# Attention over packed queries with a two-layer MLP: own PSUM tiles for copies on two engines, batch 1's p loaded apart, bias sums by 128x32 tiles, and another order of loads and work

## Chip, core and metric

The kernel runs on one core of a Trainium2 chip. The metric is the device time of one execution in microseconds (us); of the kernel before, three runs took 257.86, 258.21 and 258.63 us (median 258.21). The core has five engines that run side by side and wait for each other by semaphores: TensorE (PE, matrix products into PSUM; PEld is its loading of weights), VectorE (DVE), ScalarE (ACT), GpSimd (POOL) and SyncE (SP). Here GpSimd only makes one diagonal mask and issues loads, which turn float32 into bfloat16 on the way. SyncE issues stores and transposing transfers. In the profile "DMA" is the transfer engines.

## What is computed

There are 8 batches of 8 heads with 576 positions of 64 numbers, and 32 packed queries p per head. The packed queries attend over k and v; the 32 results of each head then serve as keys and values for q. The output, 4608 rows of 512, goes through an MLP with a squared ReLU.

```python
def sm_attn(qq, kk, vv):            # softmax(qq kk^T / 8) vv
    ...
p_packed = sm_attn(p, k, v)         # 8 x 8 x 32 x 64
x = sm_attn(q, p_packed, p_packed)  # -> 4608 x 512, heads side by side
h = x @ w_in                        # 512 -> 2048
r = np.maximum(h, 0.0)
g = s * (r * r) + b                 # s and b are single numbers
out = g @ w_out                     # 2048 -> 512
```

Since s and b are single numbers, the kernel computes `s * (r*r @ w_out) + b * colsum(w_out)`. The column sums of W_out times b are the tile `biasrep`, the same row in all 128 partitions.

## The kernel before

All products have bfloat16 operands. Every engine takes its instructions in the order in which the program names them (`Pinned`, line 67, and `mm` and `tr`, lines 61 and 64), so nearly all rows of the profile carry L62, L65 or L73, and one goes by the names of tiles. That order is a list of words written out by hand (line 609), which `run` (line 531) turns into calls. The words, with b the batch:

- `Lk`, `Lq`, `Lv`, `Lp`, `Lpall`, `Lwi`, `Lwo`, `Lsb`: loads of keys, queries, values, packed queries of batch 0, packed queries of batches 1 to 7, quarters of W_in and W_out, and s and b. All go through GpSimd's one queue, in this order. Batch 0 is loaded in halves of four heads ahead of the list (lines 586 to 596).
- `Tk`, `Tq` (`on_pe`, line 188): keys or queries of half the heads are transposed by TensorE into a PSUM tile and copied out by VectorE; for the last half of q of batch 0 ScalarE copies one half of the tile and VectorE the other. Only batches 0 and 1 go this way; later ones use a transposing transfer (`Dk`, `Dq`).
- `PD`, `PP` (`prep_p0`) and `PPA` (`prep_pall`): the packed queries are doubled, transposed and laid out block by block in `pbd`.
- `F` (`first_scores`), `V` (`order_v`), `P` (`packed`): scores of the packed queries and their exponentials, values in another order (`vr`), and the packed result with its sums in PSUM tile `pps`. At the end of the second half the result is rounded into `ppd` by four copies on two engines.
- `S`, `A`: scores of q against the packed results, exponentials `e`, and their division by their sums, which gives the weights `aT`.
- `W` (`packed_w`): the packed results times W_in, scaled into `pw`. The first MLP layer is then `aT` times `pw`. For batch 0 a word W takes one of four quarters of 512 columns.
- `M` (`mlp_in`), `h` (`mlp_in_half`): 128 columns of the first layer for a batch, or 256 for half of its rows; ReLU into `rlu` on ScalarE (a few on VectorE), squared by VectorE into `gT`.
- `B` (`bias_part`, line 437): products of W_out with a matrix of ones, added up over 16 blocks of rows; the last is multiplied by b into `biasrep`.
- `Ob.txn` (`Out.step`, line 460): n of the 16 products of output tile t, each 128x512; after the last, VectorE makes `ysb` from the sum, s and `biasrep`, and `store` (line 445) issues the stores on SyncE. The very last tile is done in two halves of columns.
- `Z` and `Y` (lines 513 and 520): products of zeros, which compute nothing.

PSUM has two pools: `psh` with two tiles of two banks (transposes, scores, first layer; rows hps) and `psy` with four tiles of one bank (outputs, packed results, batch 0's W, the bias sums, the zeros; rows yps, pps, wps, zps). A tile is free again once its last reader is done. A load waits for the landing of the load eight places earlier in GpSimd's queue, and for whatever still reads the buffer that it fills; there is one buffer each for k, q and v as loaded.

Of the kernel before, what the change touches and what calls it, by code (L numbers as in the profile page):

```python
# [14 lines left out]
def kernel(  # L15
# [79 lines left out]
    pn = constp.tile([P, 2, 2, D], BF16, name="pn")  # L95
    pall = constp.tile([16 * (B - 1), 16, 2, D], BF16, name="pall")
# [8 lines left out]
    onesb = constp.tile([P, P], BF16, name="onesb")  # L105
    zb = constp.tile([P, NB], BF16, name="zb")
# [15 lines left out]
    def load_p0():  # L122
        pool.dma_start(out=pn[:, :, 0, :], in_=p[0].rearrange("(x g) j d -> (g j) x d", x=2))

    def load_pall():
        pool.dma_start(
            out=pall[:, :, 0, :],
            in_=p[1:B].rearrange("b h (i t) d -> (b h i) t d", t=16),
        )
# [13 lines left out]
    def load_sb():  # L143
        pool.dma_start(out=svec[:], in_=moe_s[0:1].unsqueeze(0).to_broadcast([P, 1]))
        pool.dma_start(out=bvec[:], in_=moe_b[0:1].unsqueeze(0).to_broadcast([P, 1]))
# [7 lines left out]
    def prep_p0():  # L153
        pt = big(BF16)
        for x in range(2):
            tr(
                pt[:, 0, x * P:(x + 1) * P],
                pn[:, x, :, :],
                identb[:],
            )  # L160
        for c2 in range(2):
            act.copy(
                out=pbd[D * c2:D * c2 + D, :, 0, :, c2, :],
                in_=pt[D * c2:D * c2 + D, 0, 0:2 * P].rearrange("p (g a j) -> p a g j", g=4, a=2),
            )

    def prep_pall():
        twice(pall)
        n = 16 * (B - 1)
        pt = big(BF16)  # L170
        for t in range(16):
            tr(
                pt[:, t // 8, (t % 8) * P:(t % 8) * P + n],
# [3 lines left out]
        src = pt[:].rearrange("p i (t n) -> p (i t) n", n=P)[:, :, 0:n].rearrange(  # L177
            "p t (x a i) -> p a x i t", a=2, i=JJ
        )
        for c2 in range(2):  # L180
            for a in range(2):
                out = pbd[D * c2:D * c2 + D, a, 1:B, :, c2, :].rearrange("p b g (i t) -> p (b g) i t", i=JJ)
                if c2:
                    act.copy(out=out, in_=src[D * c2:D * c2 + D, a])
                else:
                    vec.tensor_copy(out=out, in_=src[D * c2:D * c2 + D, a])

    def on_pe(b, what, half):
# [3 lines left out]
        tp = big(BF16)  # L192
        for h4 in range(4):
            for cp in range(CP):
                o = (h4 % 2) * HS + cp * R
                tr(
                    tp[:, h4 // 2, o:o + R],
# [4 lines left out]
        if b == 0 and what == "q" and half == 1:  # L202
            act.copy(out=d[:, 0], in_=tp[:, 0, 0:2 * HS])
            vec.tensor_copy(out=d[:, 1], in_=tp[:, 1, 0:2 * HS])
        else:
            vec.tensor_copy(out=d, in_=tp[:, :, 0:2 * HS])
# [40 lines left out]
    def packed(b, half):  # L247
        if half == 0:
# [21 lines left out]
        if half == 0:  # L270
            return
        pd = ppd[b % 2]
        src = pp[:, 0:HP * 2 * NP].rearrange("p (g a j) -> p a g j", g=HP, a=2)
        rd[b] = smp.tile([P, 2], F32, tag="rd", name="rd")
        vec.reciprocal(out=rd[b][:], in_=sums)
        for a in range(2):
            vec.tensor_copy(out=pd[D * a:D * a + D, a], in_=src[D * a:D * a + D, a])
            act.copy(out=pd[D - D * a:2 * D - D * a, a], in_=src[D * a:D * a + D, a])
        rs[b] = smp.tile([P, 2], F32, tag="rs", name="rs")
        vec.tensor_scalar_mul(out=rs[b][:], in0=rd[b][:], scalar1=scale)  # L280
# [68 lines left out]
    def packed_w(b, chs):  # L349
        if chs[0] == 0:  # L350
# [94 lines left out]
    def store(ysb, d0, d1, i0, b, col, n):  # L445
        rows = out[b * S:(b + 1) * S, :].rearrange("(r c) d -> c r d", c=NC)
        end = i0 + n
        while i0 < end:
            x, r0 = divmod(col, R)
            m = min(R - r0, end - i0)  # L450
            sp.dma_start(out=rows[chunk(x), r0:r0 + m, d0:d1], in_=ysb[i0:i0 + m, d0:d1])
# [3 lines left out]
    class Out:  # L455
# [4 lines left out]
        def step(self, n):  # L460
# [16 lines left out]
            if m1 == NFF:  # L477
# [5 lines left out]
                for b, col, n in self.parts:  # L483
                    store(self.ysb, d0, d1, i0, b, col, n)
# [46 lines left out]
    def run(word):  # L531
# [9 lines left out]
        elif what == "Lp":  # L541
            load_p0()
# [8 lines left out]
        elif what == "PD":  # L551
            twice(pn)
        elif what == "PP":
            prep_p0()
# [12 lines left out]
        elif what == "S":  # L567
            second_scores(n[0], by_half=n[0] == 0)
# [8 lines left out]
        elif what == "O":  # L577
            if (n[0], n[1]) != (B - 1, NT):
                todo[n[0], n[1]].step(n[2])
        elif what == "B":  # L580
            bias_part(*n)


    vec.memset(zb[:], 0.0)
# [20 lines left out]
    vec.memset(onesb[:], 1.0)  # L605
    vec.memset(pbd[:, :, 1:B], 0.0)
    idle(12, NB)

    for word in """
        Lwi0 Lwi1 Lwi2 Lwi3 Lwo0 Lwo1 Lwo2 Lpall Tk0.0 Z10 PD Tk0.1 Lk1 PP0 Z3 F0.0 V0.0 F0.1 Z5 P0.0  # L610
        V0.1 P0.1 Tq0.0 Z3 Tq0.1 Lq1 Lwo3 Lv1 Lsb Z3 S0 Z2 W0.0 Z1 A0.0 Z3 W0.1 Y1 A0.1 Y1 h0.2.0 Y3
        h0.0.0 W0.2 h0.2.1 Y2 h0.0.1 M0.4 W0.3 M0.5 M0.6 M0.7 B0-4 M0.8 M0.9 O0.0x2 M0.10 B4-8 M0.11
        M0.12 O0.0x2 B8-12 M0.13 M0.14 O0.0x2 M0.15 O0.0x3 PPA Tk1.1 O0.0x3 O0.1x6 Tq1.0 O0.1x1 Tq1.1
        O0.1x1 Tk1.0 Lk2 B12-16 O0.0x1 F1.0 F1.1 O0.0x1 V1 Lv2 Lq2 O0.0x2 O0.1x3 P1.0 O0.1x1 P1.1 O0.1x4
        O0.2x1 S1 O0.2x5 A1.0 O0.2x2 A1.1 O0.2x6 W1.0 V2 O0.2x2 O0.3x8 W1.2 O0.3x3 Dq2 Dk2 Lk3 Lv3 Lq3
        O0.3x3 M1.0 O0.3x1 M1.1 O0.3x1 M1.2 O1.0x1 M1.3 M1.4 O1.0x1 M1.5 M1.6 O1.0x1 M1.7 O1.0x1 M1.8
        M1.9 O1.0x1 M1.10 O1.0x1 M1.11 O1.0x1 M1.12 O1.0x1 M1.13 O1.0x1 M1.14 O1.0x1 M1.15 O1.0x1 F2.0
        O1.0x1 F2.1 O1.0x4 O1.1x1 P2.0 O1.1x1 P2.1 O1.1x5 W2.0 O1.1x6 S2 O1.1x3 O1.2x2 A2.0 O1.2x2 A2.1
# [50 lines left out]
```

## Time and profile before

| | us |
|---|---|
| median of three runs | 258.21 |
| the profiled execution | 258.26 |
| its span in the profile | 256.1 |
| TensorE busy | 246.1 |
| VectorE, ScalarE, GpSimd busy | 143.3, 144.9, 29.6 |
| products of 128x512 for the outputs: 592 rows, busy | 145.6 |
| first layer: 512 rows of 128x288, busy | 76.4 |
| products of zeros: 49 rows, busy | 14.7 |
| bias sums: 16 rows, busy | 4.1 |

A group's row names the engine, the operation, output<-inputs, the shape, the number and the time. Busy times of TensorE overlap: a product's row includes the time until its result is in PSUM, so what counts is the step from one start to the next. Brackets give the time the engine was idle before, and whose end released it.

### The profile page before, as it was taken

How to read it: one execution, taken by the hardware profiler on the slowest of the kernel's cores; microseconds unless marked ns; L12 is line 12 of the kernel's file. 1: busy time of each engine (PE TensorE's matmuls, PEld its weight loads, DVE VectorE, ACT ScalarE, POOL GpSimd, SP SyncE). 2: the span in 40 equal slices, each digit the busy share in tenths (PEclk: the TensorE clock that was granted, in tenths of full speed). 3: DMA queues.
4: the chain of work that ended last, by engine and by line, in shares of the span. 5: the costliest groups of instructions: out<-in, count | busy, mean ns of one | idle time of the engine just before them, and what ended most of it. 6: DMA issues, size and time to landing. Idle time of an engine off the chain costs nothing.

```text
span 256.1 us, 5264 instructions
## 1 busy us (share of the span) xinstructions
PE 246.1 (96%) x2179; PEld 138.9 (54%) x2179; DVE 143.3 (56%) x271; ACT 144.9 (57%) x229; POOL 29.6 (12%) x44
## 2 busy tenths in 40 slices
PE   8988988999999999999999999999999999999994
PEld 3444546545654665456545665465546654564453
DVE  4437766658655664577365664675348634764221
ACT  2338632377958484868446855885386836782000
POOL 8633200300210003003000030002100000000000
PEclk9999999999999999999999999999999999999999
DMA  6999999897799589977981779866991931201332
GB/s 88 171 206 206 201 198 185 130 219 132 154 167 194 107 159 129 228 143 136 193 162 44 138 135 202 152 134 138 186 174 49 187 76 52 74 0 43 80 84 82
DMA packets 59208, 35.47 MB, mean 138 GB/s; under 512 B 31920, under 2 KB 54704, under 8 KB 59184
## 3 DMA queue, kind: packets, MB, share of 16 engines
q0 software_dynamic: 25232, 18.62, 49.2%
q1 hardware_dynamic: 33952, 16.52, 28.6%
q8 instruction: 17, 0.28, 0.4%
q14 instruction: 7, 0.06, 0.1%
HBM read 37.23 MB, written 9.44 MB: 182 GB/s over the span
## 4 chain that ended last, share of the span: by engine, by line
PE 80%; DMA 16%; POOL 1%; DVE 1%; issue 1%; POOLq 0%; DVEq 0%
PE yps L62 47%; PE hps L62 30%; DMA w_out_sb<-in_moe_w_out_dram 7%; DMA bvec<-in_moe_b_dram 6%; DMA vn<-in_v_dram 3%; PE pps L62 3%; POOL kn L73 1%; DVE vr L73 0%; DVE biasrep L73 0%; POOL pn L73 0%; POOL vn L73 0%; DVE ysb L73 0%; POOL identb L73 0%; POOLq L73 0%; DVEq L73 0%
## 5 line engine op out<-in xcount | busy, mean ns | idle before, releaser
L62 PE MATMUL yps<-w_out_sb,gT 128*128 128x512 bf16 (+1 forms) x592 | 145.6, 374 | 0.0
L73 ACT ACTIVATE rlu<-hps 128x576 bf16<-128x576 f32 x124 | 75.6, 648 | 26.6 <-PE hps L62 25.8
L62 PEld LDWEIGHTS <-gT 128*128 128x128 bf16 x592 | 55.0, 98 | 49.7 <-issue 6.4
L62 PE MATMUL hps<-aT,pw 128*128 128x288 bf16 x512 | 76.4, 285 | 0.6 <-ACT rlu L73 0.5
L73 DVE TENSOR_TENSOR gT<-rlu 128x576 bf16<-128x576 bf16 x128 | 57.7, 457 | 27.9 <-ACT rlu L73 24.4
L62 PEld LDWEIGHTS <-pw 128*128 128x128 bf16 x512 | 49.7, 97 | 27.6 <-issue 1.5
L73 DVE SCALAR_TENSOR_TENSOR ysb<-yps,svec,biasrep 128x512 f32<-128x512 f32 (+1 forms) x37 | 27.1, 733 | 30.1 <-PE yps L62 21.7
L73 POOL DMA_DIRECT2D kn<-in_k_dram x9 | 6.9, 766 | 135.8 <-DMA kT<-kn 94.2
L73 DVE TENSOR_TENSOR aT<-e,rcd 128x576 bf16<-128x576 bf16 x16 | 12.1, 758 | 18.4 <-ACT rcd L73 18.4
L73 ACT ACTIVATE e<-hps 96x768 bf16<-96x768 f32 x16 | 12.0, 802 | 16.0 <-PE hps L62 16.0
L73 ACT ACTIVATE pw<-hps,rd 128x1024 bf16<-128x1024 f32 x14 | 15.6, 1113 | 6.9 <-PE hps L62 6.8
L73 DVE TENSOR_SCALAR pw<-hps,rd 128x1024 bf16<-128x1024 f32 x14 | 17.9, 1278 | 2.5 <-PE hps L62 2.5
L73 ACT CAST ppd<-pps 64x128 bf16<-64x128 f32 x16 | 4.2, 260 | 17.6 <-DVE ppd L73 17.6
L62 PE MATMUL zps<-zb 128*128 128x512 bf16 x42 | 12.5, 436 | 1.2 <-DVE zb L73 1.2
L73 ACT ACTIVATE e<-hps,rs 128x576 bf16<-128x576 f32 (+1 forms) x18 | 11.4, 683 | 3.9 <-PE hps L62 3.8
L62 PEld LDWEIGHTS <-ppd 64*32 64x32 bf16 x384 | 5.3, 89 | 13.3 <-issue 12.1
L73 ACT ACTIVATE ld<-hps 128x576 f32<-128x576 f32 x16 | 10.3, 642 | 2.5 <-PE hps L62 2.0
L73 ACT ACTIVATE rcd<-ld 128x576 f32<-128x576 f32 x16 | 10.9, 683 | 0.5
L62 PE MATMUL hps<-w_in_sb,ppd 64*32 64x512 bf16 x224 | 9.8, 381 | 0.0
L73 DVE RECIPROCAL rd<-pps 128x2 f32<-128x2 f32 x8 | 1.4, 170 | 15.0 <-PE pps L62 15.0
L62 PEld LDWEIGHTS <-vr 96*128 96x128 bf16 x192 | 7.4, 97 | 3.8 <-issue 1.6
L73 ACT COPY pbd<-hps 64x256 bf16<-64x256 bf16 (+1 forms) x4 | 2.4, 633 | 11.9 <-PE hps L65 7.7
(55 smaller groups left out, 130.3 us busy)
## 6 DMA issues: line engine op xcount, KB each, us to landing
out_dram<-ysb SPq DMA_DIRECT2D x23, 192.0 KB, 2.7
kn<-in_k_dram POOLq DMA_DIRECT2D x7, 576.0 KB, 6.3
qn<-in_q_dram POOLq DMA_DIRECT2D x7, 576.0 KB, 12.0
vn<-in_v_dram POOLq DMA_DIRECT2D x7, 576.0 KB, 9.8
out_dram<-ysb SPq DMA_DIRECT2D x24, 128.0 KB, 2.4
w_in_sb<-in_moe_w_in_dram POOLq DMA_DIRECT2D x4, 512.0 KB, 13.8
w_out_sb<-in_moe_w_out_dram POOLq DMA_DIRECT2D x4, 512.0 KB, 19.2
out_dram<-ysb SPq DMA_DIRECT2D x23, 64.0 KB, 2.6
```

What stands on the lines that cost most here:

```text
L62: return tc.keep_in_program_order(nc.tensor.matmul(*a, **kw))
L73: return lambda *a, **kw: tc.keep_in_program_order(f(*a, **kw))
```

## The change

- `load_p` loads the packed queries of one batch; batches 0 and 1 are loaded so, each into a tile of its own, and the tile `pall` holds batches 2 to 7. `prep_p` is called for both. Doubling `pall` becomes a word of its own (`PA`).
- `prep_pall` transposes into two PSUM tiles of `psy` in place of one of `psh`. VectorE copies out of the first, ScalarE out of the second, four copies each.
- In `on_pe` the last half of q of batch 0 has two PSUM tiles, one for each copying engine.
- `packed` for batch 0 has one PSUM tile for each half; the first half is rounded by VectorE, the second by ScalarE, each by four copies.
- `bias_part` is replaced by `bias_sums` (word `BT`): 16 products with 32 columns of ones, each on one of four column groups of the array, so that four sums stand below each other in one PSUM tile; VectorE copies it to `biasrep`. `bias_rows` (word `BC`) multiplies it by a float32 matrix of 1/32, which adds the four, and by b.
- s and b are loaded by SyncE, first of all, in place of GpSimd.
- The second of the last half tile's two stores is issued by ScalarE.
- Loads: p of batch 1, then k, q and v of batch 1 stand ahead of the last two quarters of W_out; the rest of p comes behind them.
- The order of work is another one throughout; the words of products of zeros are Z in the same number (42) and Y in two in place of seven. Words `B` are gone. The last batch's `M` stand among products of O7.0 and O7.1.

```diff
-    pn = constp.tile([P, 2, 2, D], BF16, name="pn")
-    pall = constp.tile([16 * (B - 1), 16, 2, D], BF16, name="pall")
+    pn = [constp.tile([P, 2, 2, D], BF16, name=f"pn{i}") for i in range(2)]
+    pall = constp.tile([16 * (B - 2), 16, 2, D], BF16, name="pall")
...
+    rowsf = constp.tile([P, P], F32, name="rowsf")
...
-        pool.dma_start(out=svec[:], in_=moe_s[0:1].unsqueeze(0).to_broadcast([P, 1]))
-        pool.dma_start(out=bvec[:], in_=moe_b[0:1].unsqueeze(0).to_broadcast([P, 1]))
+        sp.dma_start(out=svec[:], in_=moe_s[0:1].unsqueeze(0).to_broadcast([P, 1]))
+        sp.dma_start(out=bvec[:], in_=moe_b[0:1].unsqueeze(0).to_broadcast([P, 1]))
...
     def prep_pall():
-        twice(pall)
-        n = 16 * (B - 1)
-        pt = big(BF16)
+        n = 16 * (B - 2)
+        pts = [psy.tile([P, 8 * P], BF16, tag="y", name="pps") for _ in range(2)]
...
+                    out = pbd[D * c2:D * c2 + D, a, 2:B, :, c2, :].rearrange(
+                        "p b g (i t) -> p (b g) i t", i=JJ
+                    )[:, :, :, 8 * x:8 * x + 8]
+                    (act.copy if x else vec.tensor_copy)(out=out, in_=src[D * c2:D * c2 + D, a])
...
-        tp = big(BF16)
+        tpw = big(BF16)
+        tp = [tpw[:, 0], tpw[:, 1]]
+        split = b == 0 and what == "q" and half == 1
+        if split:
+            tp[1] = psy.tile([P, 2 * NB], BF16, tag="y", name="tps")
...
-        if half == 0:
+
+        if half == 0 or b == 0:
             pps[b] = psy.tile([P, NB], F32, tag="y", name="pps")
...
+        if b == 0:
+            vec.reciprocal(out=rd[b][:, a:a + 1], in_=sums[:, a:a + 1])
+            gs = slice(2 * half, 2 * half + 2)
+            for a in range(2):
+                for to in (D * a, D - D * a):
+                    (act.copy if half else vec.tensor_copy)(
+                        out=pd[to:to + D, a, gs], in_=src[D * a:D * a + D, a, gs]
+                    )
...
+    def bias_sums():
+
+        ps = big()
+        for m in range(NFF):
+            r0 = NP * (m % 4)
+            mm(
+                ps[r0:r0 + NP, 0, :],
+                onesb[:, 0:NP],
+                w_out_sb[:, m, :],
+                start=(m < 4),
+                stop=(m >= NFF - 4),
+                tile_position=(0, r0),
+            )
+        vec.tensor_copy(out=biasrep[:], in_=ps[:, 0, :])
+
+    def bias_rows():
+
+        ps = big()
+        mm(ps[:, 0, :], rowsf[:], biasrep[:], start=True, stop=True)
+        vec.tensor_scalar_mul(out=biasrep[:], in0=ps[:, 0, :], scalar1=bvec[:])
...
-            sp.dma_start(out=rows[chunk(x), r0:r0 + m, d0:d1], in_=ysb[i0:i0 + m, d0:d1])
+            (other if i0 else sp).dma_start(out=rows[chunk(x), r0:r0 + m, d0:d1], in_=ysb[i0:i0 + m, d0:d1])
...
+    run("Lsb")
...
-        Lwi0 Lwi1 Lwi2 Lwi3 Lwo0 Lwo1 Lwo2 Lpall Tk0.0 Z10 PD Tk0.1 Lk1 PP0 Z3 F0.0 V0.0 F0.1 Z5 P0.0
-        V0.1 P0.1 Tq0.0 Z3 Tq0.1 Lq1 Lwo3 Lv1 Lsb Z3 S0 Z2 W0.0 Z1 A0.0 Z3 W0.1 Y1 A0.1 Y1 h0.2.0 Y3
-        h0.0.0 W0.2 h0.2.1 Y2 h0.0.1 M0.4 W0.3 M0.5 M0.6 M0.7 B0-4 M0.8 M0.9 O0.0x2 M0.10 B4-8 M0.11
-        M0.12 O0.0x2 B8-12 M0.13 M0.14 O0.0x2 M0.15 O0.0x3 PPA Tk1.1 O0.0x3 O0.1x6 Tq1.0 O0.1x1 Tq1.1
-        O0.1x1 Tk1.0 Lk2 B12-16 O0.0x1 F1.0 F1.1 O0.0x1 V1 Lv2 Lq2 O0.0x2 O0.1x3 P1.0 O0.1x1 P1.1 O0.1x4
-        O0.2x1 S1 O0.2x5 A1.0 O0.2x2 A1.1 O0.2x6 W1.0 V2 O0.2x2 O0.3x8 W1.2 O0.3x3 Dq2 Dk2 Lk3 Lv3 Lq3
+        Lwi0 Lwi1 Lwi2 Lwi3 Lwo0 Lwo1 Lp1 Tk0.0 Z10 PD Tk0.1 Lk1 PP0 Z3 F0.0 V0.0 F0.1 V0.1 Z5 P0.0 P0.1
+        Tq0.0 Z3 Tq0.1 Lq1 Lv1 Lwo2 Lwo3 Lpall Z2 S0 Z3 A0.0 W0.0 Z3 A0.1 Z1 h0.0.0 h0.2.0 W0.1 Y1
+        h0.0.1 h0.2.1 W0.2 M0.4 M0.5 Y1 M0.6 W0.3 M0.7 O0.0x4 M0.8 M0.9 PD1 O0.0x2 M0.10 M0.11 O0.0x2
+        O0.1x2 PP1 M0.12 O0.1x1 Tk1.1 Tk1.0 Lk2 O0.1x3 M0.13 O0.1x1 F1.0 O0.1x1 Tq1.1 O0.2x1 Tq1.0
+        O0.2x1 F1.1 O0.2x1 V1 Lv2 Lq2 O0.2x1 M0.14 O0.2x1 M0.15 P1.0 O0.2x1 P1.1 O0.2x1 O0.0x4 S1 O0.1x4
+        BT PA A1.0 O0.0x3 BC A1.1 O0.1x3 O0.2x3 W1.0 O0.0x1 O0.1x1 O0.2x5 W1.2 V2 O0.2x1 O0.3x5 M1.0
+        O0.3x1 M1.1 O0.3x1 M1.2 Dq2 Dk2 Lk3 Lv3 Lq3 O0.3x1 M1.3 PPA M1.4 M1.5 O0.3x8 O1.0x1 M1.6 M1.7
...
-        M7.3 M7.4 O6.2x2 M7.5 M7.6 O6.2x2 M7.7 M7.8 O6.2x2 M7.9 M7.10 O6.2x2 M7.11 M7.12 O6.2x2 M7.13
-        M7.14 O6.2x2 M7.15 O6.3x16 O7.0x16 O7.1x16 O7.2x16 O7.3x16 O7.4x16
+        A7.0 O6.1x2 A7.1 O6.1x3 O6.2x16 W7.0 O6.3x6 W7.2 O6.3x6 M7.0 O6.3x4 M7.1 M7.2 O7.0x1 O7.1x1 M7.3
+        M7.4 O7.0x2 O7.1x2 O7.0x1 O7.1x1 M7.5 M7.6 O7.0x1 O7.1x1 M7.7 M7.8 O7.0x2 O7.1x2 O7.0x1 O7.1x1
+        M7.9 O7.0x1 O7.1x1 M7.10 M7.11 O7.0x1 O7.1x1 M7.12 M7.13 O7.0x2 O7.1x2 O7.0x1 O7.1x1 M7.14 M7.15
+        O7.0x1 O7.1x1 O7.2x2 O7.0x1 O7.1x1 O7.2x1 O7.0x1 O7.1x1 O7.2x13 O7.3x16 O7.4x16
```

## The prediction

> **What bounds the kernel now.** I read the share of busy time first, then busy time by stage, then the chain that ended last, then TensorE's rows with their waits, and last the queue of load issues.
>
> ```profile
> PE 246.1 (96%) x2179; PEld 138.9 (54%) x2179; DVE 143.3 (56%) x271; ACT 144.9 (57%) x229; POOL 29.6 (12%) x44
> ```
> ```profile
> core 0: us, PE busy (x) PEld busy (x) DVE busy (x) ACT busy (x) POOL busy (x), PEclk, DMA share, GB/s
> 0.00:18.50 18.50, 15.63 (x164) 8.09 (x165) 7.66 (x24) 5.90 (x11) 11.59 (x20) 1.00 1.04 153
> 18.50:29.00 10.50, 9.05 (x80) 4.88 (x80) 8.20 (x15) 7.69 (x14) 3.45 (x5) 1.00 1.24 207
> 29.00:50.60 21.60, 19.74 (x207) 12.14 (x204) 14.52 (x26) 7.80 (x12) 3.12 (x5) 1.00 1.19 170
> 50.60:231.80 181.20, 180.98 (x1621) 102.98 (x1621) 106.93 (x199) 122.82 (x192) 11.47 (x15) 1.00 0.75 138
> 231.80:256.10 24.30, 20.74 (x112) 10.77 (x110) 6.03 (x10) 0.65 (x1) 0.00 (x0) 1.00 0.30 76
> ```
>
> From 50.6 to 231.8 us TensorE is busy 180.98 of 181.20 us. Nothing but less TensorE work can shorten that stage. What can be won lies in the first 50.6 us, where the DMA engines are full (share 1.0 to 1.2) and busy PE time is partly products of zeros, and in the 3.5 us after the last product.
>
> ```profile
> 12.21 18.64 DMA w_out_sb<-in_moe_w_out_dram
> 31.14 15.34 DMA bvec<-in_moe_b_dram
> 46.58 0.76 DVE biasrep L73
> ```
> ```profile
> 31.76 1.03 PE L62 MATMUL yps<-w_out_sb,onesb 128*128 128x512 bf16 x4
> 38.65 0.96 PE L65 MATMUL hps<-identb,pall 112*128 112x112 bf16 x16 [1.04 <-DVE pall L73]
> 42.45 0.67 PE L65 MATMUL hps<-identb,qn 96*128 96x96 bf16 x12 [0.38 <-DVE kT L73]
> 43.57 0.67 PE L65 MATMUL hps<-identb,qn 96*128 96x96 bf16 x12 [0.24 <-ACT pbd L73]
> 48.25 0.52 PE L62 MATMUL pps<-e,vr 96*128 96x64 bf16 x12 [0.20 <-DVE vr L73]
> ```
> ```profile
> 12.21 0.74 POOL L73 DMA_DIRECT2D w_out_sb<-in_moe_w_out_dram  x1 [0.71 <-DMA vn<-in_v_dram]
> 23.52 0.76 POOL L73 DMA_DIRECT2D w_out_sb<-in_moe_w_out_dram  x1 [1.50 <-DMA w_in_sb<-in_moe_w_in_dram]
> 26.33 0.78 POOL L73 DMA_DIRECT2D vn<-in_v_dram  x1 [2.05 <-DVE pw L73]
> ```
>
> The chain runs through loads up to 46.5. All loads of GpSimd share one queue and land in the order of their issue. From issue plus time to landing: first quarter of W_out 28.4, second 30.85, third 33.4, packed queries 35.2, k of batch 1 37.8, q 40.7, last quarter 43.2, v 46.2, s and b 46.3 and 46.5. The steps between are the price of a load: 2.5 for a quarter of W_out, 2.6 for k, 2.9 for q and for v, 1.75 for the packed queries, 0.16 for s or b. An issue waits for the landing of the load eight places earlier (the bracketed waits), so some eight are always under way and the queue does not run dry. The bracketed waits of TensorE between 29 and 50 sum to 1.86; with the drain of the engine in front of each I count 2.5.
>
> Steps used below: the last 112 products took 20.76 us for 80 full and 32 half ones, so 0.216 per O step; a first-MLP block M costs 0.49 (0.98 for a pair in the chain); a transposed half 0.51, a block F 0.35, half of P 0.50.
>
> **The change part by part.** *Bias.* Removed: 16 products, 3.46 us of TensorE. Added: 16 products of 128x32 tiles, four side by side. The nearest row is the scores block W, 16 products of 64x32 tiles in two waves: it starts 0.09 after the previous product would have ended, its second wave 0.23 later, and the next product 0.31 after that. Four waves: 0.09 + 3 x 0.23 + 0.31 = 1.1 (at worst no tiles beside each other, 3.7). Then one float32 product of 512 columns, for which there is no row. As a bfloat16 row it would cost 0.22[...]; by the row alone the result would be 0.7 lower. Together 2.05, so 1.4 saved. VectorE gets a copy of 0.75 and a memset of about 0.2 (a bfloat16 one of that size took 0.17), both where it idles.
>
> *s and b on SyncE, first of all.* GpSimd loses two issues (0.57 and 0.56) and two of its places. [...] By the rows, 256 tiny packets took 0.31 together, and now they stand ahead of the first keys[...]. At 1 us the engines are still empty (first keys issued 1.28, landed 5.55); I take 0.1, between 0 and 0.3.
>
> *Start of batch 0.* Before, the last half of q is copied by ScalarE (0.64), then by VectorE (0.46, waiting 0.45 for ScalarE because both read one PSUM tile); scores start at 16.78. With two tiles: half two of q lands 14.84, transposed 15.56, both copies by 16.25, scores at 16.3. p's two halves now leave PSUM apart, four small copies each on VectorE and ScalarE, done about 14.7 (15.13 before); hidden by q. A0.0 now stands before W0.0, so it no longer waits for W_in (landed 18.47): 17.7 instead of 19.08. The price is on VectorE's queue: pw of W0.0 (2 x 0.70) stands behind the weights aT, which end at 20.2, so pw is ready at 21.6 (20.4 before). The first MLP block starts 21.6, as good as unchanged (21.77), but the second half's aT is ready 22.4 instead of 23.94. Then ScalarE and VectorE set the pace through eight blocks (0.63 per relu, 0.45 per square, 0.7 per pw): M0.7 starts about 27.6, before 28.50. Five products of zeros less are covered by this wait, not by TensorE.
>
> *Loads.* Up to the second quarter of W_out nothing moves. Then come p1 (0.3), k, q, v, the two last quarters and the rest of p: p1 31.2, k 33.8, q 36.7, v 39.7, third quarter 42.2, last 44.7, p 46.2. Batch 1's loads are 4 to 6.5 us earlier, half of W_out 9 and 1.5 later.
>
> *TensorE's order.* O0.0x4 needs the first quarter (28.4): 0.3 waiting; M0.8, M0.9 end 30.25; O0.0x2 reads rows of the second quarter and waits until 30.9. This is the point that sets the rest: the start had 0.6 in hand. From there, with waits in brackets: O, M0.10, M0.11, four O, p1 transposed, M0.12, O to 34.0; Tk1.1 [0.2, its buffer is freed by ScalarE's copies of p1], Tk1.0 [0.1] 35.3; three O, M0.13, O, F1.0, O 37.3; Tq1.1 [0.1] to 37.9 (q there since 36.7); Tq1.0, F1.1 and four O to 39.6; M0.14, O, M0.15 40.8. v is reordered by 40.7, just in time for P1.0; P1.1 ends 42.05; O, O0.0x4 (third quarter, 42.2: just in time) 43.1; S1 [0.15 for ppd] 43.9; O0.1x4 44.75. BT needs the last quarter at 44.7. So every load of batch 1 is met within about 1 us, without a long wait.
>
> *Sum.* At 44.75 TensorE has done the work of before at 51.28, less two O of 33 (so 50.85), less the packed queries' transposes (0.70) and the bias (2.05). Like for like it stands at 44.75 + 2.75 = 47.5 against 50.85: 3.35 won. Against it: 0.1 for s and b, and 0.4 for small waits behind: BC's buffer, W1, and O7.0 and O7.1 now running 1.35 us behind the M7 block whose square they read, where that took 1.36 to 1.40. The split copies of p (x 96, four on ScalarE, about 0.45 each from 0.86 for 896 columns) hold ScalarE 1.7 us; nine O behind M1.5 (1.94) cover it; without them it would cost 1. The rest of the order has as many products as before, in a stage without waits: 0. Net 2.85.
>
> *The end.* The last two stores were issued one after the other by SyncE at 253.09 and 253.46 and landed 1.67 and 1.62 later. The second now goes from ScalarE's queue at 253.1: 0.3 won (0 if its first issue is slow).
>
> Total 3.15: span 256.1 to 252.95. The profiled execution took 258.26 (2.2 around the span, unchanged), so 255.1; the median of the runs, 258.21, is 0.05 below the profiled one. Forecast 255.0.
>
> **The rivals.** *The forecast*, 255.0, alone 254.4 to 255.8: 0.60.
>
> *Loads late.* v, the third and the last quarter are met with 0.1 us in hand, so each microsecond of lateness costs one. For it: those times are sums of eight prices, and a tenth of their 15 us is 1.5. Against: the same bytes in the same queue kept to these prices before. 1.5 late: 256.5. Chance 0.18.
>
> *More is won.* The waits I put at 0.6 between 31 and 45 and 0.4 behind vanish[...]: 254.1. Chance 0.15.
>
> *It saves nothing.* The tiles don't run beside each other (3.7 instead of 1.1, so 2.6 lost) and ScalarE's first store is no faster (0.3): 258.0. The W rows speak against it. Chance 0.04.
>
> *Slower: TensorE falls to half clock.* In the opening the same product of zeros steps 0.427 apart, later 0.216: there are two rates. With five fillers gone the longest pause becomes 1.25 us (20.4 to 21.6), and more follow at 26 and 30. The slow stretch of the opening lasts from 1.2 to 5.0. Each microsecond at half rate loses 0.5, so it takes 6.3 us of it inside the saturated part, nearly two such stretches, to undo the gain; three (11.4 us, 5.7 lost) would give 258.2 - 3.15 + 5.7 = 260.8. Against: the pause of 1.04 at 37.6 was followed by steps of 0.049 and 0.216. Chance 0.03.
>
> **How the numbers follow.** A change within 0.3% (0.8 us) cannot be told from none with runs that spread from 257.86 to 258.63. Faster: 0.60 + 0.18 + 0.15 = 0.93; same 0.04; slower 0.03. The range reaches from below "more is won" to above "loads late": 253.6 to 256.9, which leaves 0.07 and thin tails out.
>
> **What would show it.** Second-quarter rows of W_out wait until about 30.9; P1.0 starts near 41, BT near 45, S1 near 43.5; no wait over 0.4 after that; 16 yps products of ones gone, a block of about 1.1 and a float32 product near 0.9 in their place; last store from ScalarE. I would be wrong if v or the last quarter landed over 1 us later than 39.7 and 44.7, if a pause over 1 us stood behind 31 us, or if the stage behind 50 us showed waits.

## The result

The changed kernel takes 253.62 us, median of four runs from 253.46 to 253.97; the kernel before, run beside it, 258.12 (257.86 to 258.63). The ratio of the two is 0.9825, with an interval from 0.9806 to 0.9844: faster by 1.7%. The forecast was 255.0 with a range from 253.6 to 256.9, so the change was worth 4.5 us where 3.2 had been reckoned. The profiled execution took 253.64 us, of which the span is 251.9.

The share of busy time, then the busy time by stage. The first two rows are cut at the same times as in the table of before. The third ends inside the bias sums (before's ends at the scores of batch 1, with the bias sums done), and the fourth ends where the last 24.4 us begin.

```profile
PE 243.2 (97%) x2178; PEld 136.8 (54%) x2178; DVE 145.1 (58%) x279; ACT 145.7 (58%) x235; POOL 29.1 (12%) x43
```
```profile
core 0: us, PE busy (x) PEld busy (x) DVE busy (x) ACT busy (x) POOL busy (x), PEclk, DMA share, GB/s
0.00:18.50 18.50, 15.82 (x174) 8.21 (x174) 8.18 (x28) 6.90 (x14) 11.27 (x20) 1.00 1.05 151
18.50:29.00 10.50, 8.86 (x79) 4.67 (x72) 9.34 (x17) 7.73 (x14) 4.02 (x5) 1.00 1.25 206
29.00:45.00 16.00, 15.13 (x192) 9.57 (x193) 10.03 (x21) 7.95 (x14) 2.33 (x4) 1.00 1.39 200
45.00:227.50 182.50, 182.43 (x1619) 102.23 (x1612) 108.60 (x197) 116.50 (x183) 11.47 (x15) 1.00 0.77 142
```

TensorE still bounds the kernel, and its granted clock is 1.00 in every row, as before. (The opening products of zeros step 0.427 apart in both kernels although the row says 1.00.) Up to 29 us the rows differ little, though block M0.7 starts at 27.27 where it started at 28.50. The stage of batch 1's loads is now 16.0 us where it was 21.6, at a higher DMA share. In the long stage TensorE idles 0.07 us of 182.5. The row is longer than the 181.20 of before because it is cut earlier in the work; for the same work it became shorter, as shown below.

The chain that ended last, in order of time (start, duration, what), ran through the loads up to 46.5 before. Now it leaves them at 30.44:

```profile
4.47 7.53 DMA vn<-in_v_dram
12.29 18.15 DMA w_out_sb<-in_moe_w_out_dram
30.48 0.59 PE yps L62 x2
31.07 0.98 PE hps L62 x8
```

After that it is nearly all TensorE. Its rows between 30 and 48 us (start, duration of the group, the group, and in brackets the wait in front of it) show each step of the forecast:

```profile
30.48 0.59 PE L62 MATMUL yps<-w_out_sb,gT 128*128 128x512 bf16 x2 [0.68 <-DMA w_out_sb<-in_moe_w_out_dram]
40.57 0.52 PE L62 MATMUL pps<-e,vr 96*128 96x64 bf16 x12
42.97 0.69 PE L62 MATMUL hps<-qT,ppd 64*32 64x288 bf16 x16
44.56 1.05 PE L62 MATMUL hps<-w_out_sb,onesb 128*32 128x512 bf16 x16
45.54 0.42 PE L62 MATMUL hps<-e,onesbd 128*128 128x288 bf16 x2
46.44 1.09 PE L62 MATMUL hps<-biasrep,rowsf 128*128 128x512 f32 x2
47.37 0.41 PE L62 MATMUL hps<-e,onesbd 128*128 128x288 bf16 x2
```

O0.0x2 waits for the second quarter of W_out, and nothing behind it waits for a load. P1.0 starts at 40.57, S1 at 42.97, the tiled sums BT at 44.56, 16 products of them in a block whose next product starts 0.98 later. The float32 product stands as two rows and the next product starts 0.93 later.

**Where the 4.26 us of span went.** I place the same product in both traces. At the end of O0.1x4 TensorE stands at 44.46. The forecast's own like-for-like adds what before had done by then: 0.70 for the packed queries and the bias. The bias measures 1.09 (from the end of O0.1x4 to the row behind BT) plus 0.93. So 44.46 + 0.70 + 2.02 = 47.18 against 50.85, which is 3.67 won. From there to the first scores of batch 2 another 0.62 is won, from those to the last product 0.18 is lost, and what follows the last product's start is 0.14 shorter: 3.67 + 0.62 - 0.18 + 0.14 = 4.25. Outside the span the profiled execution has 1.77 us (253.64 - 251.87) where it had 2.13. Nothing in the trace shows these 0.36, and they stay unexplained. The experiments below narrow it down a little. The difference is 1.8 in every kernel made from the changed one, whichever engine loads s and b or issues the last store. It is also 1.8 in one made from the kernel before by moving four ReLUs alone. So neither these loads nor the last store decides it.

**The 0.62.** It lies where batch 1's first layer runs, 59 to 71 us, in the stage that the forecast called "a stage without waits". The timeline of before, ScalarE's ReLUs and TensorE's products:

```profile
60.14 11.20 ACT L73 ACTIVATE rlu<-hps 128x576 bf16<-128x576 f32 x16 [0.75 <-PE hps L62]
61.59 1.34 PE L62 MATMUL hps<-aT,pw 128*128 128x288 bf16 x8
62.98 1.33 PE L62 MATMUL hps<-aT,pw 128*128 128x288 bf16 x8
65.08 1.34 PE L62 MATMUL hps<-aT,pw 128*128 128x288 bf16 x8
```

and of after:

```profile
61.40 1.19 ACT L73 ACTIVATE rlu<-hps 128x576 bf16<-128x576 f32 x2 [0.22 <-PE hps L62]
62.15 1.14 PE L62 MATMUL hps<-aT,pw 128*128 128x288 bf16 x8
62.84 1.19 ACT L73 ACTIVATE rlu<-hps 128x576 bf16<-128x576 f32 x2 [0.25 <-PE hps L62]
63.56 1.17 PE L62 MATMUL hps<-aT,pw 128*128 128x288 bf16 x8
```

Before, ScalarE does 16 ReLUs without a gap, 0.70 each. A pair of blocks M with one O behind it is 0.98 + 0.22 = 1.20 of TensorE, and ScalarE needs 1.40 for it. TensorE gives the difference back in front of the second block: the pair's row is 1.34 instead of 1.14, three times. In the first of these rows the fourth product starts at 61.96 and the fifth at 62.28, a step of 0.32 where the others are 0.12. No wait is printed in front of those rows, for the gap of 0.2 lies between two products of one group, and a product's row lasts 0.29 on average (512 rows of 128x288), so after a step of 0.32 the engine counts as busy for nearly all of it. Behind each pair of after stand two O, 1.42 in all, and it is ScalarE that waits, 0.22 to 0.25 per pair. Three pairs at 0.2 make the 0.6. That ScalarE's rate was the cause is read from these two timelines; the experiment made for it below did not confirm it.

### The profile page after: what moved, and what is told of

Read it like the earlier page. It is cut to its first block, busy times and chain, and to the rows that moved or that the text cites. A ratio compares the mean times of both kernels' runs of the same rounds, so it can differ in the third digit from the quotient of the medians.

```text
span 251.9 us, 5279 instructions
## 1 busy us (share of the span) xinstructions
PE 243.2 (97%) x2178; PEld 136.8 (54%) x2178; DVE 145.1 (58%) x279; ACT 145.7 (58%) x235; POOL 29.1 (12%) x43
## 4 chain that ended last, share of the span: by engine, by line
PE 86%; DMA 10%; POOL 1%; issue 1%; DVE 0%; ACT 0%; POOLq 0%
PE yps L62 50%; PE hps L62 32%; DMA w_out_sb<-in_moe_w_out_dram 7%; DMA vn<-in_v_dram 3%; PE pps L62 3%; PE hps L65 1%; POOL kn L73 1%; POOL pn L73 0%; PE pps L65 0%; POOL vn L73 0%; DVE ysb L73 0%; ACT pbd L73 0%; POOL identb L73 0%; POOLq L73 0%; POOLq L701 0%
## 5 line engine op out<-in xcount | busy, mean ns | idle before, releaser
L62 PE MATMUL hps<-aT,pw 128*128 128x288 bf16 x512 | 75.4, 285 | 0.9 <-DVE pw L73 0.9
L73 DVE SCALAR_TENSOR_TENSOR ysb<-yps,svec,biasrep 128x512 f32<-128x512 f32 (+1 forms) x37 | 27.0, 733 | 21.6 <-PE yps L62 21.6
L73 DVE TENSOR_TENSOR aT<-e,rcd 128x576 bf16<-128x576 bf16 x16 | 12.1, 757 | 21.6 <-ACT rcd L73 21.5
L73 ACT CAST ppd<-pps 64x128 bf16<-64x128 f32 (+1 forms) x18 | 4.5, 248 | 18.1 <-DVE ppd L73 16.1
L73 ACT ACTIVATE rcd<-ld 128x576 f32<-128x576 f32 x16 | 10.9, 683 | 0.5
L73 DVE COPY vr<-vn 96x3072 bf16<-96x3072 bf16 (+1 forms) x9 | 7.7, 861 | 1.3 <-DMA vn<-in_v_dram 1.2
L62 PE MATMUL pps<-e,vr 96*128 96x64 bf16 x192 | 8.2, 192 | 0.2 <-ACT e L73 0.2
```

The source lines that it names most:

```text
L62: return tc.keep_in_program_order(nc.tensor.matmul(*a, **kw))
L73: return lambda *a, **kw: tc.keep_in_program_order(f(*a, **kw))
```

## The experiments

The kernels were measured in three sets. Those of one set ran side by side on one chip with the kernel before, and only they are set against each other. Ratios are to the kernel before.

### First set: the bias, the PSUM tiles, the loads

*The old bias in the new order.* The sixteen full products stand where BT stood; the float32 product is gone.

```diff
-            r0 = NP * (m % 4)
-            mm(
-                ps[r0:r0 + NP, 0, :],
-                onesb[:, 0:NP],
...
-        vec.tensor_copy(out=biasrep[:], in_=ps[:, 0, :])
+            mm(ps[:, 0, :], onesb[:], w_out_sb[:, m, :], start=(m == 0), stop=(m == NFF - 1))
+        vec.tensor_scalar_mul(out=biasrep[:], in0=ps[:, 0, :], scalar1=bvec[:])
...
-        BT PA A1.0 O0.0x3 BC A1.1 ...
+        BT PA A1.0 O0.0x3 A1.1 ...
```

> The changed kernel with the bias sums made as before: 16 full products of 128x512 at the place of the tiled ones, no float32 product. Theory: TensorE is saturated from 45 us on, so its steps count in full. The tiled products and the float32 one took 1.09 and 0.93 us in the changed kernel, the 16 old ones 3.45: slower than the changed kernel by 1.4 us, 255.0. Rival (the gain lies in the start alone, the bias products are hidden by waits there): no difference, 253.6.

Measured: 256.6 (256.40 to 259.1), ratio 0.9969 (0.9953 to 0.9985).

*The new bias in the old order.* BT stands in the place of the last four bias products, BC five products later (three of them O0.1); the three earlier groups of four are taken out.

```diff
...
-        h0.0.0 W0.2 h0.2.1 Y2 h0.0.1 M0.4 W0.3 M0.5 M0.6 M0.7 B0-4 M0.8 M0.9 O0.0x2 M0.10 B4-8 M0.11
-        M0.12 O0.0x2 B8-12 M0.13 M0.14
+        h0.0.0 W0.2 h0.2.1 Y2 h0.0.1 M0.4 W0.3 M0.5 M0.6 M0.7 M0.8 M0.9 O0.0x2 M0.10 M0.11
+        M0.12 O0.0x2 M0.13 M0.14
...
-        O0.1x1 Tk1.0 Lk2 B12-16 O0.0x1 F1.0 F1.1 O0.0x1 V1 Lv2 Lq2 O0.0x2 O0.1x3 P1.0
+        O0.1x1 Tk1.0 Lk2 BT O0.0x1 F1.0 F1.1 O0.0x1 V1 Lv2 Lq2 O0.1x3 BC O0.0x2 P1.0
```

> The kernel before with only the bias sums changed (tiled products at the place of the last four old ones, the float32 product three output products later). Theory: 3.45 us of products go, 2.0 come, so 1.4 faster than before, 256.7; if the new place costs a wait for PSUM tiles of the scores, 257.0. Rival (three of the four old groups lie in a stage that waits for loads anyway): under 0.7 faster, 257.5 or more.

Measured: 257.69, ratio 0.999 (0.9982 to 0.9997).

*One PSUM tile again.* The last half of q and the two halves of p of batch 0 share a tile as before.

```diff
-        split = b == 0 and what == "q" and half == 1
+        split = False
...
-        if split:
+        if b == 0 and what == "q" and half == 1:
...
-        if half == 0 or b == 0:
+        if half == 0:
...
-        if b == 0:
+        if False:
```

> The changed kernel with the copies of batch 0 from shared PSUM tiles again (last half of q in one tile, the packed results of batch 0 in one tile and rounded at the end of the second half). Theory: the start has some 0.7 us in hand, the wait for the second quarter of W_out at 29.8. The scores of batch 0 start about 0.7 later (16.5 instead of 15.85) and that wait shrinks by as much: 253.6 to 253.8. Rival (the start's chain decides): slower by the whole 0.7, 254.3.

Measured: 255.01 (254.94 to 256.63), ratio 0.9906 (0.9883 to 0.993).

*A third quarter ahead.* The third quarter of W_out is loaded ahead of batch 1's loads again.

```diff
-        Lwi0 Lwi1 Lwi2 Lwi3 Lwo0 Lwo1 Lp1 Tk0.0 ...
+        Lwi0 Lwi1 Lwi2 Lwi3 Lwo0 Lwo1 Lwo2 Lp1 Tk0.0 ...
...
-        Tq0.0 Z3 Tq0.1 Lq1 Lv1 Lwo2 Lwo3 Lpall ...
+        Tq0.0 Z3 Tq0.1 Lq1 Lv1 Lwo3 Lpall ...
```

> The changed kernel with the third quarter of W_out loaded ahead of p, k, q and v of batch 1; the order of work stays. Theory: p, k, q and v land 2.5 us later and were met with 0.4 (k) and 0.3 (v) us in hand, so TensorE stands about 2.1 us longer: 255.7. Rival (the order of TensorE's work makes the gain and has room for loads): under 0.5 slower, 254.1.

Measured: 256.81, ratio 0.9967 (0.9953 to 0.998).

**What the first set says.** The bias. The old one costs 256.6 - 255.0 = 1.6 more in the new order, against 1.4 forecast and 3.46 - 2.02 = 1.44 from the traces. (The changed kernel itself was not in this set, so the kernel with shared tiles stands for it. In both, and in the kernel with a third quarter ahead, the times fall into groups some 1 to 2.5 us apart at granted clocks from 0.985 to 1.00; the third set shows how such a step comes about. Counting only the times at a clock above 0.995, the medians are 256.52 and 254.97, 1.55 apart.) In the trace the old products form one row, and the next product starts 3.46 later:

```profile
46.70 3.62 PE L62 MATMUL hps<-w_out_sb,onesb 128*128 128x512 bf16 x16
50.16 0.41 PE L62 MATMUL hps<-e,onesbd 128*128 128x288 bf16 x2
```

In the old order the same saving is nearly worthless: 0.1 us, and the spans do not differ at all (medians 255.8, and 255.7 before). TensorE's timeline shows what came in its place:

```profile
27.93 0.65 PE L62 MATMUL hps<-aT,pw 128*128 128x288 bf16 x4 [0.47 <-ACT rlu L73]
29.09 1.14 PE L62 MATMUL hps<-aT,pw 128*128 128x288 bf16 x8 [0.51 <-DVE rlu L73]
32.18 0.65 PE L62 MATMUL hps<-aT,pw 128*128 128x288 bf16 x4 [0.51 <-DVE rlu L73]
50.04 0.70 PE L62 MATMUL hps<-qT,ppd 64*32 64x288 bf16 x16
```

and the same two places, M0.7 and S1, in the kernel before:

```profile
28.50 0.65 PE L62 MATMUL hps<-aT,pw 128*128 128x288 bf16 x4 [0.47 <-ACT rlu L73]
50.65 0.69 PE L62 MATMUL hps<-qT,ppd 64*32 64x288 bf16 x16
```

The twelve products taken out had filled the time in which the blocks M wait for a free PSUM tile, that is, for ReLUs of ScalarE and VectorE. Without them TensorE waits there. This profile is 0.57 ahead already at M0.7, in front of the first product taken out, because its W_in landed earlier. The 2.59 us of the twelve raise that lead by only 1.22 up to the transposes of the packed queries (36.86 where before has 38.65). By P1.0 BT and BC, which stand in the place of four products, have used up 1.18 of it. At S1 the lead is 0.61, so of the 1.4 nothing to speak of is left. The bias saving is real only where the order has other work for those places, which the forecast had not asked. The new loads and the new order were not tried apart from each other.

The PSUM tiles. 255.01 cannot be set against 253.62, which was not measured in this set. One cause of the difference shows in the trace: here the first keys landed at 7.43, in the changed kernel's profile at 5.96. The kernel with the last store on SyncE, below, has the changed kernel's tiles, and its keys landed at 7.45. With shared tiles M0.7 starts 0.55 later (29.21 against 28.66), but the other kernel then waits 0.46 for the second quarter of W_out and this one does not, so both are level behind it: F1.0 at 37.50 and 37.55, last product at 249.27 and 249.32. Their medians differ by 0.3, and they are of two sets, so what can be said is that the traces show no gain from the tiles of their own. That is what the forecast had in its prices, since it put the first MLP block "as good as unchanged".

The order of the loads. One quarter ahead of batch 1 costs 256.81 - 255.01 = 1.8. Against the kernel with shared tiles k and v land 2.4 later (36.66 for 34.31, 42.51 for 40.11), and TensorE waits for k:

```profile
34.73 0.27 PE L65 MATMUL hps<-identb,pn 128*128 128x128 bf16 x2 [0.62 <-DVE rlu L73]
36.71 1.19 PE L65 MATMUL hps<-identb,kn 96*128 96x96 bf16 x24 [0.99 <-DMA kn<-in_k_dram]
```

That 2.4 of lateness costs 1.8 and not 2.4 is the slack that the loads had: without the edit TensorE meets k 0.7 after it lands (Tk1.1 starts at 34.97).

### Second set: s and b, the fillers, ScalarE, the last store

*s and b by GpSimd, last.* As in the kernel before.

```diff
-        sp.dma_start(out=svec[:], in_=moe_s[0:1].unsqueeze(0).to_broadcast([P, 1]))
-        sp.dma_start(out=bvec[:], in_=moe_b[0:1].unsqueeze(0).to_broadcast([P, 1]))
+        pool.dma_start(out=svec[:], in_=moe_s[0:1].unsqueeze(0).to_broadcast([P, 1]))
+        pool.dma_start(out=bvec[:], in_=moe_b[0:1].unsqueeze(0).to_broadcast([P, 1]))
...
-    run("Lsb")
...
-        Tq0.0 Z3 Tq0.1 Lq1 Lv1 Lwo2 Lwo3 Lpall ...
+        Tq0.0 Z3 Tq0.1 Lq1 Lv1 Lwo2 Lwo3 Lpall Lsb ...
```

> The changed kernel with s and b loaded by GpSimd again, as its last loads ahead of batch 2's. Theory: moving them was worth nothing: they land at 46, two microseconds before the first use, and the first keys may land up to 0.4 us earlier (5.96 in the changed kernel, 5.55 before), which the wait for the second quarter of W_out swallows unless that lands earlier too: 253.4 to 253.8. Rival (the two places in GpSimd's queue count): slower by 0.5 or more.

Measured: 254.07 (253.68 to 254.46), ratio 0.9853 (0.9838 to 0.9868).

*No fillers behind the first keys.* 22 products of zeros are taken out of the start of batch 0; the first ten are kept.

```diff
-        ... Z10 PD Tk0.1 Lk1 PP0 Z3 F0.0 V0.0 F0.1 V0.1 Z5 P0.0 P0.1
-        Tq0.0 Z3 Tq0.1 ...
+        ... Z10 PD Tk0.1 Lk1 PP0 F0.0 V0.0 F0.1 V0.1 P0.0 P0.1
+        Tq0.0 Tq0.1 ...
...
-        ... Z2 S0 Z3 A0.0 W0.0 Z3 A0.1 Z1 h0.0.0 h0.2.0 W0.1 Y1
-        h0.0.1 h0.2.1 W0.2 M0.4 M0.5 Y1 M0.6 ...
+        ... S0 A0.0 W0.0 A0.1 h0.0.0 h0.2.0 W0.1
+        h0.0.1 h0.2.1 W0.2 M0.4 M0.5 M0.6 ...
```

> The changed kernel without the 22 products of zeros that stand behind the first keys' transposes (they compute nothing). Forecast's theory: they lie in waits, so the time stays within 0.3 us: 253.4 to 253.9. Rival (half clock): TensorE has long pauses from 9 to 22 us, its steps for 512 columns rise from 0.216 to 0.427 for a stretch, and each microsecond of it inside work costs 0.5; with the start's 0.7 in hand, 254.5 to 257.

Measured: 256.09 (255.0 to 257.07), ratio 0.993 (0.9909 to 0.9951).

*ScalarE relieved in the kernel before.* Four of batch 1's sixteen ReLUs go to VectorE, as four of batch 0's do already.

```diff
-        if b == 0 and m % 4 == 2:
+        if b <= 1 and m % 4 == 2:
```

> The kernel before with four of batch 1's sixteen ReLUs on VectorE instead of ScalarE. Theory (new, from the two traces): in that stretch, 60 to 71 us, ScalarE ran its ReLUs without a pause, 16 in 11.2 us, and TensorE lost 0.5 to 0.6 us in steps of 0.32 instead of 0.12 that its busy share doesn't show; with 4 x 0.65 us less on ScalarE that is won: 257.6. Rival (TensorE bounds that stage, as the prediction had it): no change, 258.1.

Measured: 259.21 (259.12 to 259.64), ratio 1.0057 (1.0044 to 1.007).

*The last store from SyncE.*

```diff
-                    store(self.ysb, d0, d1, i0, b, col, n, act if d0 else sp)
+                    store(self.ysb, d0, d1, i0, b, col, n)
```

> The changed kernel with the very last store on SyncE again. Theory: the store issued by ScalarE landed 1.91 us after its issue, one by SyncE would be issued 0.37 later and land after 1.6: 0.1 us slower, so 253.6 to 253.8. Rival (the prediction's value): 0.3 slower, 253.9. The time around the span (1.8 us in the changed kernel, 2.1 before) would grow by 0.3 if the second store queue has to do with it.

Measured: 254.71 (254.57 to 254.80), ratio 0.9876 (0.9861 to 0.9891).

**What the second set says.** The fillers. The kernel without them must be set against the one with SyncE's last store, which issues s and b alike and whose first keys come equally late: 1.4 us slower. The windows from 4 to 15 and from 15 to 30 us, first without fillers, then with them (the first number behind the five pairs is the granted clock, PEclk):

```profile
4.00:15.00 11.00, 7.33 (x105) 4.63 (x104) 3.51 (x9) 2.24 (x4) 7.66 (x11) 1.00 1.23 178
15.00:30.00 15.00, 10.95 (x95) 5.20 (x93) 8.83 (x19) 9.86 (x20) 4.84 (x6) 0.66 1.26 205
```
```profile
4.00:15.00 11.00, 9.65 (x113) 5.32 (x112) 3.48 (x9) 2.23 (x4) 7.63 (x11) 1.00 1.23 178
15.00:30.00 15.00, 12.63 (x128) 6.43 (x125) 10.95 (x23) 11.08 (x22) 4.84 (x6) 1.00 1.26 206
```

Without fillers the granted clock between 15 and 30 us is 0.66. From 18.8 us the products step at half rate, after five pauses of 0.41 to 1.24 us since 10.9. The blocks M run at half rate: eight products of a pair take 2.10 (at 25.36) where the kernel with fillers takes 1.14. The fillers compute nothing, and with them the granted clock in that window is 1.00. This is the mechanism of the rival that was to end on the slow side. In the profile of the changed kernel, with five fillers fewer than before, it did not come: the clock is 1.00 in every row.

ScalarE. Relieving it made the kernel before 1.3 us slower (1.6 by the span), where half a microsecond had been expected to be won. VectorE takes its work in order, and a ReLU there stands behind an output's sum (ysb) or a square, as the timeline of both engines shows:

```profile
61.32 0.75 DVE L73 SCALAR_TENSOR_TENSOR ysb<-yps,svec,biasrep 128x512 f32<-128x512 f32 x1
61.99 0.75 DVE L73 TENSOR_SCALAR rlu<-hps 128x576 bf16<-128x576 f32 x1
...
62.38 0.65 PE L62 MATMUL hps<-aT,pw 128*128 128x288 bf16 x4 [0.74 <-ACT rlu L73]
...
65.63 1.14 PE L62 MATMUL hps<-aT,pw 128*128 128x288 bf16 x8 [0.29 <-DVE rlu L73]
```

So a second engine at the same PSUM tiles was a new wait, 0.29 in the last row above. This run does not show that ScalarE's rate had been the limit; that rests on the two timelines above, the ReLUs without a gap and the steps of 0.32 where 0.12 is the usual one.

s and b. With GpSimd the kernel takes 254.07, with SyncE and SyncE's last store 254.71. The two differ in two parts, so the third set takes the question apart. The first keys land at 5.57 here and at 7.45 there.

### Third set: the changed kernel again, s and b, float32

*The changed kernel again.* No edit; it is the base of this set.

> The changed kernel once more, beside the others of this call. In the runs with s and b first on SyncE the first keys landed at 7.4 us, in its own first profile at 5.96; before, at 5.55. Theory: the two small loads can hold the first keys up by up to 1.9 us, and what exceeds the start's 0.7 in hand shows: 254.6 where the keys land at 7.4, 253.6 where they land at 6.0. Rival (the other runs were slow by their own edits): 253.6 wherever it runs.

Measured: 255.35 (254.24 to 255.95), ratio 0.9896 (0.9873 to 0.9918). The times fall into two groups: 254.24, 254.68, 254.81 at a granted clock of 1.00 and 255.89, 255.92, 255.95 at 0.99.

*s and b by GpSimd, last.* The kernel of the second set, now beside the changed kernel.

```diff
...
-    run("Lsb")
...
-        Tq0.0 Z3 Tq0.1 Lq1 Lv1 Lwo2 Lwo3 Lpall ...
+        Tq0.0 Z3 Tq0.1 Lq1 Lv1 Lwo2 Lwo3 Lpall Lsb ...
```

> The changed kernel with s and b as GpSimd's last loads ahead of batch 2's, once more. Theory: first keys at 5.6 us, 253.6 to 254.1, some 0.6 faster than the changed kernel on the same chip if that has its keys at 7.4. Rival (no effect of the small loads): the same as the changed kernel within 0.2.

Measured: 253.97 (253.53 to 254.07), ratio 0.9848 (0.9835 to 0.9861).

*A bfloat16 product in place of the float32 one.* It starts from the kernel just named. The four sums and the matrix of 1/32 are rounded to bfloat16.

```diff
-    rowsf = constp.tile([P, P], F32, name="rowsf")
+    rowsf = constp.tile([P, P], BF16, name="rowsf")
+    biasq = constp.tile([P, NB], BF16, name="biasq")
...
-        vec.tensor_copy(out=biasrep[:], in_=ps[:, 0, :])
+        vec.tensor_copy(out=biasq[:], in_=ps[:, 0, :])
...
-        mm(ps[:, 0, :], rowsf[:], biasrep[:], start=True, stop=True)
+        mm(ps[:, 0, :], rowsf[:], biasq[:], start=True, stop=True)
```

> As sb_pool2, with the four bias sums rounded to bfloat16 and added up by a bfloat16 product instead of the float32 one. Theory ([...]the float32 product stood as two rows of 0.50 and 0.43 us): 0.93 becomes 0.22, so 0.7 faster than sb_pool2, 253.0 to 253.3. Rival (what follows waits for VectorE's copy and for batch 1's weights, not for TensorE): under 0.2 faster.

Measured: 254.03 (253.85 to 254.21), ratio 0.9855 (0.984 to 0.9869).

*The kernel before with s and b on SyncE, first of all.*

```diff
-        pool.dma_start(out=svec[:], in_=moe_s[0:1].unsqueeze(0).to_broadcast([P, 1]))
-        pool.dma_start(out=bvec[:], in_=moe_b[0:1].unsqueeze(0).to_broadcast([P, 1]))
+        sp.dma_start(out=svec[:], in_=moe_s[0:1].unsqueeze(0).to_broadcast([P, 1]))
+        sp.dma_start(out=bvec[:], in_=moe_b[0:1].unsqueeze(0).to_broadcast([P, 1]))
...
+    run("Lsb")
     vec.memset(zb[:], 0.0)
...
-        ... Tq0.0 Z3 Tq0.1 Lq1 Lwo3 Lv1 Lsb Z3 S0 ...
+        ... Tq0.0 Z3 Tq0.1 Lq1 Lwo3 Lv1 Z3 S0 ...
```

> The kernel before with s and b loaded by SyncE first of all, nothing else. Theory: its first keys land later than 5.55 us, up to 7.4, its start has up to 1.4 us of waits for W_in in hand, and bvec, which landed at 46.5 and held up biasrep, is there at once: between 0.3 faster and 0.6 slower than before. Rival (the small loads cost nothing and the wait for bvec counts): 0.3 or more faster with first keys at 5.6.

Measured: 258.15, ratio 1.0031 (1.0017 to 1.0044). Fifteen of 22 runs lie between 258.10 and 258.19, six between 259.77 and 259.87.

**What the third set says.** TensorE's opening rows, first of the changed kernel in one of its longer executions (255.89), then with s and b by GpSimd:

```profile
7.51 1.05 PE L65 MATMUL hps<-identb,kn 96*128 96x96 bf16 x12 [2.07 <-DMA kn<-in_k_dram]
8.36 3.66 PE L62 MATMUL zps<-zb 128*128 128x512 bf16 x10
```
```profile
6.24 0.68 PE L65 MATMUL hps<-identb,kn 96*128 96x96 bf16 x12
6.75 2.32 PE L62 MATMUL zps<-zb 128*128 128x512 bf16 x10
```

Two costs can be read. The keys are 1.9 us later when s and b go first on SyncE. By itself that makes the kernel slower by 0.7 (254.24 to 254.81, median 254.68, against 253.97); the start's slack takes the rest. The kernel before loses 0.3 by the same edit, 258.15 against 257.83. And behind a pause of 2 us TensorE is at half rate: ten products of zeros take 3.66 where they take 2.32, until about 11.3 us. That is another 1.2 in the runs in which it happens. Here the pause is long because the last of the twelve products of zeros ahead of it were already at full rate and ended early (4.25 us for the twelve, against 5.20). The two came together in every profile with the half rate, so which of them decides is not separated.

Where the 1.9 come from is half shown. The share of the DMA engines in 40 slices of the first 8.5 us, first a kernel with s and b on SyncE (the one with SyncE's last store), then with them on GpSimd:

```profile
DMA  0000000000000000000483984699999999999999
```
```profile
DMA  0000000000000975699999999999999999999999
```

The engines are not busy with s and b, which are 128 times 4 bytes each; they are idle. The keys' packets start at 4.2 us instead of 2.8, though the keys are issued at the same time. So it is not the time of their packets, from which the forecast took its 0.1. In the profile of the result the packets started at 2.8 us and the keys were only 0.4 late, with the same instructions. What decides between 0.4 and 1.9 was not found.

The float32 product. The bfloat16 one costs 0.25 instead of 0.93, and the kernel does not gain (254.03 against 253.97). TensorE's timeline shows the time that came free as a wait before W1:

```profile
46.75 0.38 PE L62 MATMUL hps<-biasq,rowsf 128*128 128x512 bf16 x1
48.63 0.39 PE L62 MATMUL hps<-w_in_sb,ppd 64*32 64x512 bf16 x1
49.17 0.62 PE L62 MATMUL hps<-w_in_sb,ppd 64*32 64x512 bf16 x15 [0.15 <-DVE biasrep L73]
```

W1's second product starts at 49.17, in the kernel with float32 at 49.21. The engine stands until VectorE has made biasrep, whose PSUM tile W1 is to take over. The 0.68 by which the float32 product is dearer is hidden, and the forecast's alternative "by the row alone the result would be 0.7 lower" does not hold even where the product is that cheap.

**A version that beats both.** With s and b on GpSimd's queue, last, the changed kernel takes 253.97 where it takes 255.35 itself on the same chip, and its times do not fall into two groups. The result's 253.62 was measured apart from this set, with the keys only 0.4 late; the two numbers do not stand against each other.

## Why the prediction was right, and what it missed

The change is faster for the reasons forecast, but that the time lies inside the range is in part luck. 253.62 is 0.02 above its lower end, and the same kernel took 254.24 to 255.95 when it was measured again, with the first keys later. The forecast reckoned with neither that spread nor the gain in the long stage.

*The bound.* Right. TensorE was saturated behind 50 us, and the loads of batch 1 set the end before that. The chain left the loads at 30.44, and one quarter of W_out moved back ahead of batch 1 costs 1.8.

*Bias.* Right in its sizes. The tiled products took 1.09 where four waves were reckoned at 1.1, so the row of the scores block was the right neighbour. The float32 product took 0.93 where 0.95 was taken, an estimate of the author's that no row of before shows; the bfloat16 row, 0.22, would have been wrong by 0.7. But the saving of 1.4 was counted at its full size without naming what it leans on. It holds in the new order, which is where it was measured as 1.6, and is lost to other waits in the old one.

*s and b on SyncE.* The term was mis-sized: 0.1, between 0 and 0.3. The first keys came 0.4 later in the profile of the result and 1.9 later in all seven other profiles with this edit. The upper bound came from the time of the packets; what counts is a delay in which the engines are idle (their share is 0 up to 4.0 us in the view of the third set, where the keys' packets start at 4.2). In the result it cost nothing visible, since the start had 0.6 in hand.

*Start of batch 0.* Right. S0 at 15.85 (forecast 16.3), A0.0 at 17.43 (17.7), M0.7 at 27.27 (27.6). As forecast the start has slack, which is why the PSUM tiles show no gain.

*Loads.* Right in order, and 0.2 to 0.4 early: the second quarter of W_out landed at 30.44 (30.85), k at 33.41 (33.8), q at 36.32 (36.7), v at 39.28 (39.7), the third quarter at 41.80 (42.2), the last at 44.48 (44.7). The lead exists already at the first quarter (27.8 for 28.4), up to the second of which "nothing moves" had been said. By its size it is the part of the gain that was not reckoned: 3.67 for 3.35. The forecast took the landings of one profile as fixed. Two experiments that keep the loads of the kernel before had the second quarter at 30.5 and 30.3, where its own profile had 30.85. So the lead is within what differs from one execution to the next, and it is no property of the change: in the later profiles with late keys k lands at 34.03 and 34.31, behind the forecast, and those kernels take 254.7 and 255.0, near the forecast's time.

*The rest.* This step failed. The forecast took off 0.4 "for small waits behind" and put the rest of the order, "a stage without waits", at 0. The waits of 0.4 were not there, and the stage had hidden ones before: 0.62 won and 0.18 lost, so +0.44 where -0.4 stood. A busy share of 180.98 of 181.20 had been read as proof that no time is lost. It shows only that the rows of products overlap: a row of 128x288 lasts 0.29 where the step is 0.12, so most of a step of 0.32 counts as busy. The steps from one product's start to the next would have told it.

*The end.* Too large: 0.3 forecast, 0.14 found, and nothing in the time. SyncE's and ScalarE's issues both stand at 248.97, and ScalarE's store takes 1.91 to land where SyncE's takes 1.75. The kernel with SyncE's last store ends as soon after its last product's start (3.7) as the changed one, so the 0.14 is not ScalarE's doing.

*Sum.* 3.67 for 3.35, +0.44 for -0.4, 0.14 for 0.3 and 0.1 not charged make 4.25 where 3.15 stood, so the span is 1.1 lower; 0.36 outside the span is the rest of the 1.46 between 255.1 and 253.64, the profiled execution.

*The rivals.* The case that came is "more is won", given 0.15 and 254.1, and only in part for its reason: the 0.4 of waits behind did vanish, but the rest came from the loads' lead, from hidden waits of before and from the 0.36 outside the span, which that rival did not name. "Loads late" had its mechanism shown by the third quarter ahead; the loads themselves were on time. "Half clock" is a real price: 1.4 without the fillers, 1.2 behind late keys, but far from the 5.7 that would have been needed. "Saves nothing" fell with the 1.09.

## What to carry to other kernels

Work taken off the bounding engine is a gain only if other work is ready for its place: the same saving was worth 1.6 us in one order and next to nothing in another. On a saturated engine read the steps from start to start and not the busy share, and look how each group of products is balanced against the engine that empties its PSUM tiles (by the two timelines here, two O per pair of blocks M, where one left ScalarE behind). Keep products of zeros where the engine would pause (here 1.4 us were lost without 22 of them), and small early loads away from the front of the first large load (0.7 lost here), until a trace shows that they cost nothing.

## What the runs showed of the hardware

Two broadcast loads of 128 times 4 bytes on SyncE, issued at 0.74 and 1.21 us ahead of GpSimd's first load at 1.3, delayed that load's first packet from 2.8 to 4.2 us in seven of eight profiles, with the DMA engines idle meanwhile.

TensorE fell to half rate after pauses of 1.89, 1.98 and 2.07 us in front of the first keys (the ten products of zeros behind them took 4.01, 3.80 and 3.66 us), and not after pauses of 0.98 to 1.60 in four others (2.32 us). Five pauses of 0.41 to 1.24 us within 8 us, in the kernel without fillers, were followed by the same (granted clock 0.66 from 15 to 30 us).

A float32 product of 512 columns stands in the trace as two rows and costs 0.93 us, against 0.25 for the bfloat16 one in its place.
